# Reordering the attention blocks and the last product of a retention + mixture-of-experts kernel

## The chip, the cores and the metric

One core of one Trainium2 chip. The time is the device time of one execution in microseconds (us), median of several runs; lower is better. Distances inside an execution are taken from the start times in its trace.

## The reference

```python
def _attn_ref(q, k, v):                        # (8, 8, 576, 64) each
    scores = scale * np.matmul(q, k.transpose(0, 1, 3, 2))
    # Dmat[h, i, j] = gamma_h ** (i - j) for i >= j, else 0
    return np.matmul(scores * Dmat[None], v)

def _moe_ref(x, domain_probs, w1, w2):         # x: (4608, 512), 4 experts, F = 1024
    p = domain_probs / (domain_probs.sum(-1, keepdims=True) + 1e-09)
    out = 0
    for e in range(E):
        out += p[:, e:e + 1] * (np.maximum(x @ w1[e], 0.0) @ w2[e])
    return out
```

The result of attention, with its heads side by side, is the x of the experts.

## The kernel before

Attention is computed in chunks of 128 tokens with carried states: for a "duo" of two head pairs, `kv` builds the states of chunks from k^T v, `scores` the products inside a chunk, and `values` the output o, from the duo's own scores and from the states. A block takes the new duo's `kv` and `scores` and the old duo's `values`, so that VectorE and ScalarE have time between them. Blocks are set between the matmuls of the experts; ph is the result tile of their first layer, pd that of their second. The last 64 of the 576 tokens, the remainder, have products of their own (sr is the tile of their scores). A tile shape such as 128*64 is the rows and columns of TensorE's array that a matmul uses. Every result tile comes from one ring of four PSUM slots, two banks each.

```python
ring = ctx.enter_context(tc.tile_pool(name="ring", bufs=4, space=PSUM))
# ... class Duo:
def kv(self):
    kvp = ring_tile("kvp", [128, 2, NC, D])
    # ... 16 matmuls, tiles of 128*64: kvp += k^T v
    for j in range(2):
        r = slice(64 * j, 64 * j + 64)
        nc.scalar.activation(sbd[r, self.ps, :, r], kvp[r], Copy)     # the states
def scores(self):
    for i, p in self.pairs():
        s = ring_tile("s", [128, 2, NC, C])
        # ... 8 matmuls, tiles of 64*128; then one multiplication on VectorE: s -> sT
def values(self):
    o = ring_tile("o", [128, 2, SM])
    for i, p in self.pairs():                                         # own values, 128*64
        for c in range(NC):
            for j in range(2):
                nc.tensor.matmul(o[64*j:64*j+64, i, c*C:(c+1)*C], lhsT=bv[p][:, c, j, :],
                                 rhs=self.sT[p][:, j, c, :], start=(c == 0), stop=False, ...)
    for i, p in self.pairs():                                         # carried states, 128*128
        for c in range(1, NC):
            nc.tensor.matmul(o[:, i, c*C:(c+1)*C], lhsT=sbd[:, p, c-1, :],
                             rhs=self.qT[p][:, c, :], start=False, stop=(c == NC - 1), ...)
    # ... ScalarE copies o into xt, in two pieces
def block(new, old):
    if new is not None: new.kv()
    if old is not None: old.values()
    if new is not None: new.scores()
```

There are twelve duos: ten blocks with an old and a new duo, two with a new one only, two with an old one only.

The experts' second product goes by seven products and some sums for each group of 256 tokens. Its four result parts X, Y, W, Z lie in one ring tile `pd`: X and Y in one bank, W and Z in the other. The output rows of the group's second half are W + Y + p1 (left) and Y + p1 + p5 (right), with p1 and p5 copies of partial results.

```python
for m in (1, 4, 2, 5, 6, 3, 7):                # order of the products, every group
    d[s].product(m)
# ... in product(n), for the very last group:
elif n == 3:
    # ...
    if self.last:
        nc.gpsimd.tensor_tensor(self.p5, self.p5, self.p1, op=ADD)
        rd.append(nc.vector.tensor_tensor(self.ob[:, 0:HF], W, self.p1, op=ADD))
elif n == 7 and self.last:                     # both halves wait for Y, the last product
    nc.vector.tensor_tensor(self.ob[:, 0:HF], Y, self.ob[:, 0:HF], op=ADD)
    nc.sync.dma_start(out=out[n0 + 128:n0 + 256, 0:HF], in_=self.ob[:, 0:HF])
    nc.vector.tensor_tensor(self.ob[:, HF:Dm], Y, self.p5, op=ADD)
    nc.scalar.dma_start(out=out[n0 + 128:n0 + 256, HF:Dm], in_=self.ob[:, HF:Dm])
```

Of the kernel before, what the change touches and what calls it, by code (L numbers as in the profile page):

```python
# [9 lines left out]
FP32 = mybir.dt.float32  # L10
# [5 lines left out]
ADD = mybir.AluOpType.add  # L16
# [7 lines left out]
def kernel(  # L24
# [10 lines left out]
    nc = tc.nc  # L35
    B, H, S, D = q.shape
    N, E = moe_domain_probs.shape
    _, Dm, F = moe_w1.shape
    assert (B, H, S, D) == (8, 8, 576, 64) and (N, E, Dm, F) == (4608, 4, 512, 1024)
    scale = 1.0 / math.sqrt(D)  # L40
    C = 128
    NC = 4
# [7 lines left out]
    HF = Dm // 2  # L50
# [10 lines left out]
    opool = ctx.enter_context(tc.tile_pool(name="opool", bufs=2))  # L61
    tpool = ctx.enter_context(tc.tile_pool(name="tpool", bufs=1))
# [3 lines left out]
    def ring_tile(name, shape, dt=FP32):  # L66
        return ring.tile(shape, dt, tag="ring", name=name)
# [23 lines left out]
    sbd = const.tile([128, NP, NC, 128], BF16, name="sbd")  # L91
# [133 lines left out]
    def xt_of(t):  # L225
        if t not in xt:
            xt[t] = xpool.tile([128, NDC, NT], BF16, tag="xt", name="xt")
        return xt[t]


    class Duo:
        def __init__(self, b, d):
            self.b, self.d = b, d
            self.ps = slice(2 * d, 2 * d + 2)
            self.qT, self.kT, self.sT = {}, {}, {}
# [39 lines left out]
        def values(self):  # L275
            o = ring_tile("o", [128, 2, SM])
            for i, p in self.pairs():
                for c in range(NC):
                    for j in range(2):
                        nc.tensor.matmul(o[64 * j:64 * j + 64, i, c * C:(c + 1) * C], lhsT=bv[p][:, c, j, :],  # L280
                                         rhs=self.sT[p][:, j, c, :], start=(c == 0), stop=False, skip_group_check=True)
            for i, p in self.pairs():
                for c in range(1, NC):
                    nc.tensor.matmul(o[:, i, c * C:(c + 1) * C], lhsT=sbd[:, p, c - 1, :], rhs=self.qT[p][:, c, :],  # L284
                                     start=False, stop=(c == NC - 1), skip_group_check=True)
            n0 = self.b * S
            a = 0
            while a < SM:
                t = (n0 + a) // NT
                z = min(SM, (t + 1) * NT - n0)  # L290
                nc.scalar.activation(xt_of(t)[:, self.ps, n0 + a - t * NT:n0 + z - t * NT], o[:, :, a:z], Copy)
                a = z

    def block(new, old):
        if new is not None:
            new.kv()
        if old is not None:
            old.values()
        if new is not None:
            new.scores()  # L300


# [120 lines left out]
    class Down:  # L423


        def __init__(self, h, t, s):
            self.h, self.t, self.s = h, t, s
            self.last = t == n_nt - 1 and s == 1
            self.reads = [[], []]
            self.a = slice(256 * s, 256 * s + 128)  # L430
            self.b = slice(256 * s + 128, 256 * s + 256)

# [17 lines left out]
        def product(self, n):  # L450
            h = self.h
            if n == 1:
                self.ps = ring_tile("pd", [128, 2, 2, HF])
            X, Y, W, Z = (self.ps[:, 0, 0], self.ps[:, 0, 1], self.ps[:, 1, 0], self.ps[:, 1, 1])
            lo = range(KH)
            hi = range(KH, 2 * KH)
            A = {1: (X, True, h, lo, self.a, lambda c: wx[0][:, c, 0]),
                 2: (X, False, h, hi, self.a, lambda c: wx[1][:, c, 0]),
                 3: (Z, False, getattr(self, "s4", None), lo, slice(0, 128), lambda c: wx[1][:, c, 1]),
                 4: (W, True, h, hi, self.b, lambda c: t4w[:, c]),  # L460
                 5: (Z, True, getattr(self, "s1", None), lo, slice(0, 128), lambda c: wx[0][:, c, 1]),
                 6: (Y, True, getattr(self, "s2", None), lo, slice(0, 128), lambda c: t2w[:, c]),
                 7: (Y, False, h, lo, self.b, lambda c: t3w[:, c])}
            dst, start, src, ks, tok, rhs = A[n]
            bank = 0 if n in (1, 2, 6, 7) else 1
            for c, kk in enumerate(ks):
                mm = nc.tensor.matmul(dst, lhsT=src[:, kk, tok], rhs=rhs(c), start=(start and c == 0),  # L467
                                      stop=(c == KH - 1), skip_group_check=True)
                for r in self.reads[1 - bank]:
                    tc.declare_no_dep(mm.ins, r.ins, reason="another bank of the same tile")  # L470
            rd = self.reads[bank]
            n0 = self.t * NT + 256 * self.s
            if n == 1:
                self.p1 = tpool.tile([128, HF], FP32, tag="p1", name="p1")
                rd.append(nc.scalar.activation(self.p1, X, Copy))  # L475
            elif n == 2:
                self.oa = opool.tile([128, Dm], FP32, tag="o", name="oa")
                rd.append(nc.scalar.activation(self.oa[:, 0:HF], X, Copy))
            elif n == 5:
                self.p5 = tpool.tile([128, HF], FP32, tag="p5", name="p5")  # L480
                rd.append(nc.scalar.activation(self.p5, Z, Copy))
            elif n == 6:
                self.u = tpool.tile([128, HF], FP32, tag="uv", name="u")
                rd.append(nc.vector.tensor_tensor(self.u, Y, self.p1, op=ADD))  # L484
            elif n == 3:
                rd.append(nc.vector.tensor_tensor(self.oa[:, HF:Dm], Z, self.u, op=ADD))
                nc.sync.dma_start(out=out[n0:n0 + 128, :], in_=self.oa)
                if self.last:
                    self.ob = opool.tile([128, Dm], FP32, tag="o", name="ob")
                    nc.gpsimd.tensor_tensor(self.p5, self.p5, self.p1, op=ADD)  # L490
                    rd.append(nc.vector.tensor_tensor(self.ob[:, 0:HF], W, self.p1, op=ADD))
            elif n == 7 and self.last:
                nc.vector.tensor_tensor(self.ob[:, 0:HF], Y, self.ob[:, 0:HF], op=ADD)
                nc.sync.dma_start(out=out[n0 + 128:n0 + 256, 0:HF], in_=self.ob[:, 0:HF])
                nc.vector.tensor_tensor(self.ob[:, HF:Dm], Y, self.p5, op=ADD)
                nc.scalar.dma_start(out=out[n0 + 128:n0 + 256, HF:Dm], in_=self.ob[:, HF:Dm])
            elif n == 7:
                self.v = tpool.tile([128, HF], FP32, tag="uv", name="v")
                nc.vector.tensor_tensor(self.v, Y, self.p1, op=ADD)  # L499
                self.ob = opool.tile([128, Dm], FP32, tag="o", name="ob")  # L500
                nc.vector.tensor_tensor(self.ob[:, 0:HF], W, self.v, op=ADD)
                nc.gpsimd.tensor_tensor(self.ob[:, HF:Dm], self.v, self.p5, op=ADD)  # L502
                nc.sync.dma_start(out=out[n0 + 128:n0 + 256, :], in_=self.ob)
# [232 lines left out]
    def run(slots, i):  # L736
        for f in slots.get(i, []):
            f()

    slots = {}  # L740
    add = lambda i, f: slots.setdefault(i, []).append(f)
# [30 lines left out]
    n = 0  # L772
# [17 lines left out]
    NS = 30  # L790
# [5 lines left out]
    for b in range(2, B):  # L796
# [21 lines left out]
        for at, f in ((rem_at[1], rem.cast), (rem_at[1], rem.trans_dma), (rem_at[2], rem.scores), (rem_at[3], rem.values)):  # L818
            add(at, f)
    add(NS * 5 + 13, lambda old=old: block(None, old))  # L820

    for t in range(1, n_nt):
        d = [Down(h, t, s) for s in range(2)]
        for s in range(2):
            for i, which in enumerate((1, 2, 4, 3)):
                for lo in (0, KH // 2):
                    add(NS * (t - 1) + 16 + 7 * s + i,
                        lambda s=s, which=which, lo=lo, d=d: d[s].sums(which, lo, lo + KH // 2))
        n = NS * (t - 1)
        for e in range(E):  # L830
            for i in range(4):
                up_group(h, t, e, i)
                run(slots, n)
                n += 1
        for s in range(2):
            for m in (1, 4, 2, 5, 6, 3, 7):
                d[s].product(m)
                run(slots, n)
                n += 1
# [30 lines left out]
```

## Time and profile before

| kernel before | |
|---|---|
| time, median of 3 runs | 535.93 us (535.61 to 535.97) |
| profiled span | 533.7 us |
| a block: from the start of the expert matmul before it to the start of the one after it | 2.432 us (8 of the ten blocks) |
| the same where it stands between products of the second expert layer | 2.325 us (2 blocks) |
| first k^T v to last matmul | 421.67 us |
| tail: start of the last matmul to the end of the span | 3.96 us |

The two blocks between second-layer products are shorter because a matmul there is followed after 109 ns, not 216. The next lines are the chain of work that ended last, in order of time, around one block of before (start, length, engine, tile, line, count).

```profile
377.10 0.68 PE kvp L255 x16
377.78 0.45 PE o L280 x16
378.23 0.44 PE o L284 x6
378.67 0.55 PE s L269 x16
379.23 0.32 PE ph L359
```

### The profile page before, as it was taken

To read this page: it belongs to the slowest core of one execution; us is meant where nothing else is said; L and a number is where in the kernel's file an instruction comes from. 1 tells how busy PE (TensorE), PEld (TensorE's weight loads), DVE (VectorE), ACT (ScalarE), POOL (GpSimd) and SP (SyncE) were. 2 spreads that over 40 slices of the span, in tenths; PEclk is the share of its full clock that TensorE was granted. 3 is DMA by queue.
4 is the path that set the end of the run, shared out by engine and by line. 5 is a ranking of instruction groups with operands and counts; after the bars stand their busy time and mean duration, and the time that the engine had idled before them with its cause. 6 is when DMAs were issued, how large, how long until landed. Compare 5 with 4: busy or idle time off the path is not lost.

```text
span 533.7 us, 10188 instructions
## 1 busy us (share of the span) xinstructions
PE 525.1 (98%) x4221; PEld 340.4 (64%) x4260; DVE 362.1 (68%) x456; ACT 87.2 (16%) x175; POOL 147.1 (28%) x188
## 2 busy tenths in 40 slices
PE   8999999999999999999999999999999999999997
PEld 4644544478745885478646865587548844884586
DVE  5426668895577667697578767776765566556754
ACT  4723440012101111020101101100110000000010
POOL 5734104245235434336132514063000000000000
PEclk9999999999999999999999999999999999999999
DMA  9999947878769866937363655454011111110001
GB/s 238 208 212 251 238 116 190 166 164 168 155 146 170 169 139 146 165 73 164 106 136 93 142 140 115 104 120 124 20 41 31 50 39 41 41 46 14 1 32 49
DMA packets 145118, 63.55 MB, mean 119 GB/s; under 512 B 124240, under 2 KB 135888, under 8 KB 145072
## 3 DMA queue, kind: packets, MB, share of 16 engines
q1 hardware_dynamic: 134752, 43.50, 36.9%
q0 software_dynamic: 10176, 19.27, 16.5%
q8 instruction: 33, 0.54, 0.4%
q10 hardware_dynamic: 144, 0.13, 0.1%
q14 instruction: 13, 0.11, 0.1%
HBM read 53.56 MB, written 9.51 MB: 118 GB/s over the span
## 4 chain that ended last, share of the span: by engine, by line
PE 96%; DVE 1%; ACT 1%; DMA 1%; issue 1%; SPq 0%; DVEq 0%
PE ph L359 46%; PE pd L467 37%; PE po L394 5%; PE kvp L255 1%; PE o L280 1%; PE s L269 1%; PE o L284 1%; PE ph L380 1%; DMA raw_0q<-in_q_dram 1%; PE kvp L574 1%; PE w L138 1%; DVE h L365 0%; PE o L619 0%; ACT sbd L594 0%; PE pt L533 0%
## 5 line engine op out<-in xcount | busy, mean ns | idle before, releaser
L359 PE MATMUL ph<-xt,w 128*128 128x512 bf16 x1102 | 249.1, 379 | 2.0 <-DVE h L365 0.2
L365 DVE SCALAR_TENSOR_TENSOR h<-ph,pB 128x1024 bf16<-128x1024 f32 x128 | 156.5, 1224 | 56.9 <-PE ph L359 56.1
L359 PEld LDWEIGHTS <-w 128*128 128x128 bf16 x1136 | 109.3, 98 | 127.5
L467 PEld LDWEIGHTS <-h 128*128 128x128 bf16 x1024 | 99.8, 98 | 13.2
L467 PEld LDWEIGHTS <-s 128*128 128x128 bf16 x768 | 75.1, 98 | 8.6
L467 PE MATMUL pd<-wx,h 128*128 128x256 bf16 x512 | 61.1, 273 | 0.0
L467 PE MATMUL pd<-wx,s 128*128 128x256 bf16 x512 | 61.1, 273 | 0.0
L220 POOL DMA_DIRECT2D pB<-pd x28 | 15.8, 565 | 150.3 <-DVE h L365 134.7
L502 POOL TENSOR_TENSOR ob<-v,p 128x256 f32<-128x256 f32 x15 | 12.3, 822 | 114.2 <-DVE v L499 85.5
L239 POOL TENSOR_TENSOR bf_k<-raw_k,gk 128x512 bf16<-128x512 f32 x24 | 26.1, 1086 | 35.3 <-DMA raw_k<-in_k_dram 21.6
L260 ACT ACTIVATE sbd<-kvp 64x512 bf16<-64x512 f32 x24 | 14.2, 592 | 121.5 <-PE kvp L255 121.3
L271 DVE TENSOR_TENSOR sT<-s,tri 128x1024 bf16<-128x1024 f32 x24 | 28.3, 1219 | 7.5 <-PE s L269 7.5
L467 PE MATMUL pd<-t3w,h 128*128 128x256 bf16 x256 | 30.6, 273 | 0.0
L467 PE MATMUL pd<-t4w,h 128*128 128x256 bf16 x256 | 30.6, 273 | 0.0
L467 PE MATMUL pd<-t2w,s 128*128 128x256 bf16 x256 | 30.6, 273 | 0.0
L444 DVE TENSOR_TENSOR s<-s,h 128x1024 bf16<-128x1024 bf16 x32 | 29.6, 966 | 0.0
L394 PE MATMUL po<-wx,h 128*128 128x512 bf16 x124 | 28.6, 379 | 0.3 <-issue 0.2
L475 ACT ACTIVATE p<-pd 128x256 f32<-128x256 f32 x16 | 6.1, 384 | 138.9 <-PE pd L467 113.1
L239 POOL TENSOR_TENSOR bf_q<-raw_q,gq 128x512 bf16<-128x512 f32 x24 | 27.2, 1135 | 2.1 <-DMA raw_q<-in_q_dram 1.7
L448 DVE TENSOR_TENSOR s<-h,s 128x1024 bf16<-128x1024 bf16 x32 | 27.3, 891 | 0.0
L442 DVE TENSOR_TENSOR s<-h 128x1024 bf16<-128x1024 bf16 x32 | 23.5, 775 | 0.0
L484 DVE TENSOR_TENSOR u<-pd,p 128x256 f32<-128x256 f32 x16 | 6.8, 425 | 23.4 <-PE pd L467 23.3
(156 smaller groups left out, 370.2 us busy)
## 6 DMA issues: line engine op xcount, KB each, us to landing
pB<-pd POOLq DMA_DIRECT2D x28, 256.0 KB, 3.7
raw_k<-in_k_dram SPq DMA_DIRECT2D x48, 128.0 KB, 2.9
raw_q<-in_q_dram SPq DMA_DIRECT2D x48, 128.0 KB, 3.1
raw_v<-in_v_dram SPq DMA_DIRECT2D x48, 128.0 KB, 3.1
wx<-in_moe_w_dram POOLq DMA_DIRECT2D x4, 1024.0 KB, 15.4
out_dram<-oa SPq DMA_DIRECT2D x16, 256.0 KB, 2.2
out_dram<-ob SPq DMA_DIRECT2D x15, 256.0 KB, 2.2
w<-in_moe_w_dram POOLq DMA_DIRECT2D x3, 1024.0 KB, 15.1
```

What stands on the lines that cost most here:

```text
L220: eng.dma_start(out=pB[t, e], in_=pd[e:e + 1, t * NT:(t + 1) * NT].to_broadcast([128, NT]))
L239: eng.tensor_tensor(bfs[p % 2][n], raw1[n], g[:, :, 2 * p:2 * p + 2].unsqueeze(3).to_broadcast([128, NC, 2, D]), op=MULT)
L260: nc.scalar.activation(sbd[r, self.ps, :, r], kvp[r], Copy)
L271: nc.vector.tensor_tensor(sT[:, :, :, :].rearrange("p j c t -> p (j c) t"), s[:, :, :, :].rearrange("p j c t -> p (j c) t"), tri[:, :].uns ...
L359: nc.tensor.matmul(ph[:, f, :], lhsT=w1_sb[e][:, dc, fc * 128:(fc + 1) * 128], rhs=x[:, dc, :], start=(dc == 0), stop=(dc == NDC - 1))
L365: nc.vector.scalar_tensor_tensor(h[:, fk:fk + 2, :], ph, 0.0, pB[t, e][:, :].unsqueeze(1).to_broadcast([128, 2, NT]), op0=MAX, op1=MULT)
L394: nc.tensor.matmul(po[:, g, :], lhsT=h[:, e * NFC + fc, ns * 128:(ns + 1) * 128], rhs=wx[e // 2][:, (e % 2) * NFC + fc, :, :].rearrange("p ...
L442: nc.vector.tensor_tensor(self.alloc("s1")[:, l], h[:, l, self.b], h[:, r, self.b], op=ADD)
L444: nc.vector.tensor_tensor(self.alloc("s2")[:, l], self.s1[:, l], h[:, l, self.a], op=SUB)
L448: nc.vector.tensor_tensor(self.alloc("s4")[:, l], h[:, r, self.a], self.s2[:, l], op=SUB)
L467: mm = nc.tensor.matmul(dst, lhsT=src[:, kk, tok], rhs=rhs(c), start=(start and c == 0), stop=(c == KH - 1), skip_group_check=True)
L502: nc.gpsimd.tensor_tensor(self.ob[:, HF:Dm], self.v, self.p5, op=ADD)
```

## The change

The intent has two parts. In a block, let the states go first, since they have the tile shape of the expert matmuls before them: three changes of shape in place of four. At the very end, let the last product feed one half of one output only, so that one addition and one store follow it.

```diff
         def values(self):
             o = ring_tile("o", [128, 2, SM])
             for i, p in self.pairs():
+                for c in range(1, NC):
+                    nc.tensor.matmul(o[:, i, c * C:(c + 1) * C], lhsT=sbd[:, p, c - 1, :], rhs=self.qT[p][:, c, :],
+                                     start=(c == 1), stop=False, skip_group_check=True)
+            for i, p in self.pairs():
                 for c in range(NC):
                     for j in range(2):
                         nc.tensor.matmul(o[64 * j:64 * j + 64, i, c * C:(c + 1) * C], lhsT=bv[p][:, c, j, :],
-                                         rhs=self.sT[p][:, j, c, :], start=(c == 0), stop=False, skip_group_check=True)
-            for i, p in self.pairs():
-                for c in range(1, NC):
-                    ...
+                                         rhs=self.sT[p][:, j, c, :], start=False, stop=(c == NC - 1),
+                                         skip_group_check=True)
     def block(new, old):
-        if new is not None:
-            new.kv()
         if old is not None:
             old.values()
         if new is not None:
+            new.kv()
             new.scores()
# ... Down.product, last group only: Y in a ring tile of its own
+                if self.last:
+                    self.py = ring_tile("py", [128, HF])
+            if self.last:
+                Y = self.py
# ... the additions
-                if self.last:
-                    (GpSimd addition p5 + p1, VectorE addition W + p1)
             elif n == 7 and self.last:
-                (two additions of Y, each with a store)
+                self.v = tpool.tile([128, HF], FP32, tag="uv", name="v")
+                rd.append(nc.vector.tensor_tensor(self.v, Y, self.p1, op=ADD))
+                self.ob = opool.tile([128, Dm], FP32, tag="o", name="ob")
+                nc.vector.tensor_tensor(self.ob[:, HF:Dm], self.v, self.p5, op=ADD)
+                nc.scalar.dma_start(out=out[n0 + 128:n0 + 256, HF:Dm], in_=self.ob[:, HF:Dm])
+            elif n == 4 and self.last:
+                nc.vector.tensor_tensor(self.ob[:, 0:HF], W, self.v, op=ADD)
                 nc.sync.dma_start(out=out[n0 + 128:n0 + 256, 0:HF], in_=self.ob[:, 0:HF])
# ... the first sum of the last group three slots earlier, and the order of its products
-                    add(NS * (t - 1) + 16 + 7 * s + i,
+                    add(NS * (t - 1) + 16 + 7 * s + i - (3 if d[s].last and i == 0 else 0),
-            for m in (1, 4, 2, 5, 6, 3, 7):
+            for m in (1, 5, 2, 6, 3, 7, 4) if d[s].last else (1, 4, 2, 5, 6, 3, 7):
```

More of the change, by code (lines that the diff above doesn't have):

```diff
@@ L280, in values @@
                         nc.tensor.matmul(o[64 * j:64 * j + 64, i, c * C:(c + 1) * C], lhsT=bv[p][:, c, j, :],
-                                         rhs=self.sT[p][:, j, c, :], start=(c == 0), stop=False, skip_group_check=True)
-            for i, p in self.pairs():
-                for c in range(1, NC):
-                    nc.tensor.matmul(o[:, i, c * C:(c + 1) * C], lhsT=sbd[:, p, c - 1, :], rhs=self.qT[p][:, c, :],
-                                     start=False, stop=(c == NC - 1), skip_group_check=True)
+                                         rhs=self.sT[p][:, j, c, :], start=False, stop=(c == NC - 1),
+                                         skip_group_check=True)
             n0 = self.b * S
@@ L428, in __init__ @@
             self.last = t == n_nt - 1 and s == 1
-            self.reads = [[], []]
+            self.reads = [[], [], []]
             self.a = slice(256 * s, 256 * s + 128)
@@ L464, in product @@
             dst, start, src, ks, tok, rhs = A[n]
-            bank = 0 if n in (1, 2, 6, 7) else 1
+            bank = 2 if self.last and n in (6, 7) else 0 if n in (1, 2, 6, 7) else 1
             for c, kk in enumerate(ks):
@@ L468, in product @@
                                       stop=(c == KH - 1), skip_group_check=True)
-                for r in self.reads[1 - bank]:
+                for r in self.reads[1 - bank] if bank < 2 else ():
                     tc.declare_no_dep(mm.ins, r.ins, reason="another bank of the same tile")
@@ L487, in product @@
                 nc.sync.dma_start(out=out[n0:n0 + 128, :], in_=self.oa)
-                if self.last:
-                    self.ob = opool.tile([128, Dm], FP32, tag="o", name="ob")
-                    nc.gpsimd.tensor_tensor(self.p5, self.p5, self.p1, op=ADD)
-                    rd.append(nc.vector.tensor_tensor(self.ob[:, 0:HF], W, self.p1, op=ADD))
             elif n == 7 and self.last:
-                nc.vector.tensor_tensor(self.ob[:, 0:HF], Y, self.ob[:, 0:HF], op=ADD)
+                self.v = tpool.tile([128, HF], FP32, tag="uv", name="v")
[5 more added lines that the diff above has]
+                nc.vector.tensor_tensor(self.ob[:, 0:HF], W, self.v, op=ADD)
                 nc.sync.dma_start(out=out[n0 + 128:n0 + 256, 0:HF], in_=self.ob[:, 0:HF])
-                nc.vector.tensor_tensor(self.ob[:, HF:Dm], Y, self.p5, op=ADD)
-                nc.scalar.dma_start(out=out[n0 + 128:n0 + 256, HF:Dm], in_=self.ob[:, HF:Dm])
             elif n == 7:
```

## The prediction

> **What bounds the kernel now.** I read the page first (busy shares, then the chain that ended last), then the timeline of one block of attention products, then the last microseconds.
>
> ```profile
> PE 525.1 (98%) x4221; PEld 340.4 (64%) x4260; DVE 362.1 (68%) x456; ACT 87.2 (16%) x175; POOL 147.1 (28%) x188
> PE 96%; DVE 1%; ACT 1%; DMA 1%; issue 1%; SPq 0%; DVEq 0%
> ```
>
> TensorE (PE) is busy 98% and carries 96% of the chain. So only what shortens PE's stream, or the piece after its last matmul, can count. The number and shapes of the matmuls do not change; their order does. The next view is PE's timeline around one full block (columns: start, length, engine, line, operation, names, tile, shape, count).
>
> ```profile
> 376.29 0.81 PE L359 MATMUL ph<-xt,w 128*128 128x512 bf16 x3
> 377.03 0.75 PE L255 MATMUL kvp<-v,bf_k 128*64 128x256 bf16 x16
> 377.61 0.62 PE L280 MATMUL o<-sT,bf_v 128*64 128x128 bf16 x16
> 378.16 0.51 PE L284 MATMUL o<-qT,sbd 128*128 128x128 bf16 x6
> 378.60 0.62 PE L269 MATMUL s<-qT,kT 64*128 64x128 bf16 x16
> 379.16 0.39 PE L359 MATMUL ph<-xt,w 128*128 128x512 bf16 x1
> ```
>
> The reader is to see the tile column: 128*128, then 128*64 (k^T v and own values), then 128*128 (carried states), then 64*128 (scores), then 128*128: four changes of tile shape per block. In the trace's start times the matmul after each change comes late: k^T v 309 ns after a matmul that is otherwise followed after 216; states 151 after a pair usually 53 apart from the next; scores 152 after one usually 56; the next ph 148 after 53. Each change costs 93 to 98 ns, and the second step after it about 11 more. ScalarE (ACT) in the same block:
>
> ```profile
> 377.82 1.20 ACT L260 ACTIVATE sbd<-kvp 64x512 bf16<-64x512 f32 x2 [12.38 <-PE kvp L255]
> 379.04 1.08 ACT L291 ACTIVATE xt<-o 128x128 bf16<-128x128 f32 x2
> ```
>
> It first copies kvp into the state (done 379.02), then o into xt (done 380.13). PE's next ph at 379.16 is not held by either; note how narrow that is. How soon PE restarts on a released buffer is in two views, VectorE (DVE), then PE:
>
> ```profile
> 108.26 1.22 DVE L365 SCALAR_TENSOR_TENSOR h<-ph,pB 128x1024 bf16<-128x1024 f32 x1 [0.27 <-PE ph L359]
> ```
>
> ```profile
> 109.53 1.24 PE L359 MATMUL ph<-xt,w 128*128 128x512 bf16 x5 [0.15 <-DVE h L365]
> ```
>
> DVE ends at 109.483, PE starts at 109.535: 52 ns (other such places: 52 to 57). The end of the run, DVE, SyncE queue, ACT queue and DMA issues:
>
> ```profile
> 530.06 0.42 DVE L493 TENSOR_TENSOR ob<-pd,ob 128x256 f32<-128x256 f32 x1 [0.99 <-PE pd L467]
> 530.40 0.41 DVE L495 TENSOR_TENSOR ob<-pd,p 128x256 f32<-128x256 f32 x1
> ```
>
> ```profile
> 530.51 0.33 SPq L494 DMA_DIRECT2D out_dram<-ob  x1
> ```
>
> ```profile
> 530.85 0.37 ACTq L496 DMA_DIRECT2D out_dram<-ob  x1
> ```
>
> ```profile
> out_dram<-ob SPq DMA_DIRECT2D x1, 128.0 KB, 1.7
> out_dram<-ob ACTq DMA_DIRECT2D x1, 128.0 KB, 1.8
> ```
>
> Two half-row additions follow the last matmul, one after the other, each with its own 128 KB store. The second, issued at 530.85, lands near 532.6; about 1.1 us of closing work takes the span to 533.7.
>
> **What the Trainium skill says.** "TensorEngine Tiling (Array Packing)", Key Properties: changing the tiling mode (not just the tile) drains TensorE. The trace agrees and gives the price: 93 to 98 ns at each change, next to nothing between two products of one shape. "PSUM — Partial Sum Buffer", The four PSUM rules: the first matmul of a group clears the written-bits of a whole bank over the quadrants it writes, and later ones without that flag overwrite where the bit is clear. That makes the new start flags right: the states go first with start on chunk 1, and own values of chunk 0 then overwrite. No time is in it. "Perfetto Trace Analysis", Identifying the Most-Contended Engine: busy share says little about a pipelined TensorE; so I count start-to-start gaps, which the uneven gaps above support. Same page, DMA Instruction — HWDGE: a transfer's movement is not in the issuing instruction, and the final descriptor's wait for the write can be long; here 1.7 to 1.8 us from issue to landing.
>
> **The change, part by part.**
>
> 1. Order inside a block. New order: states (128*128), own values (128*64), k^T v (128*64), scores (64*128). The first shape is that of the product before the block, so three changes stay of four. Ten blocks have both an old and a new duo (twelve duos; two blocks have only a new one, two only an old one). From the old ph: states first at 0.216, last 5 x 56 ns later, 0.496; own values first at +0.149, 0.645, last 0.419 later, as in the old-only block at 396.9, 1.064; k^T v first 1.117, last 0.533 later, 1.650; scores first at +0.125, 1.775, last at +0.405, 2.180; next ph possible at +0.148, 2.328. Before it was 2.432 (376.725 to 379.157). Saved if nothing waits: 0.104 us, ten times 1.04 us.
>
> 2. But the blocks also allocate o before kvp now. The ring of result tiles has four slots and a block takes four (o, kvp, s, s), so the first product after it needs the slot that was kvp's and is now o's. The list of waits in the two built programs confirms it: the first ph after a block waited for the state copy and now waits for the second xt copy. o's last matmul starts at 1.064; in old-only blocks xt's copy starts 0.256 later (1.320); the two copies take 1.085 in every split (2.405); PE restarts 0.054 later: 2.459. That is 131 ns after the 2.328 where it could go, and 27 after the old 2.432. The slow second step (about 10 ns) is hidden by the wait. So a full block costs about +0.017 us instead of saving 0.104; ten give +0.17 us. Where a block sits between products of the down stage the next product also takes a ring slot: same sum. The state copies now end near 3.6, but the second ph after the block needs that slot only at about 2.46 + 8 x 0.216 = 4.19: no wait.
>
> 3. Old-only blocks (two): changes stay at two; about 0.015 us less each: -0.03.
>
> 4. Tail. The last product now feeds only W, so one addition of 0.42 us follows it and one store; Y's half is finished during the last product. The last store is issued where the first one was (530.51), not at 530.85. In the trace the first store is seen landed at 532.25, the second at 532.62: 0.37 us earlier. Y's own bank and the moved sums cost PE nothing, if the sums come in time: product 5 starts at 519.38 and its sum, moved up three slots, is done near 516.5; product 7 starts at 526.37 and its difference, queued behind an addition ending near 525.3, takes two halves of 0.64: first half 525.95, needed 526.37; second half 526.6, needed 527.24. The GpSimd addition that goes (0.73 us) was off the path.
>
> Sum: +0.17 - 0.03 - 0.37 = -0.23, so 535.93 becomes 535.70 us.
>
> **The rivals.** (a) The wait does not bind: 1.04 us from blocks, 0.37 from the tail, 0.03: 534.5. For it: ACT is only 16% busy. Against: the program's waits name the xt copy, and from o's last start to a free slot and a restarted PE it is 0.256 + 1.085 + 0.054 = 1.395 us, while PE has only 0.053 + 0.533 + 0.125 + 0.405 + 0.148 = 1.264 us of other work to do. (b) Something else stalls more: the scores now come 0.1 us sooner and need a slot that a DVE group frees. At 376.7 that group ends at 378.37, the second scores would start near 378.70; margin 0.3. If it bound, or the copies of ACT ran late, each block would lose 0.1 more: 536.7. (c) The tail's difference comes late and product 7 waits: up to 0.4 us, eating the tail's gain: 536.1. Against it the margins 0.4 and 0.6 above. (d) The first store was hidden by the closing work anyway: no gain in the tail, 536.1; against: the last SyncE waits follow the second landing directly.
>
> **Range and chances.** Between my sum and rival (a) lie 1.2 us, 0.2%; the three runs of before spread by 0.36. I take 535.7, with 534.9 to 536.1 eight times in ten; the lower side is longer for a part of (a). 2% would be 10.7 us, far beyond every rival: within 2% 0.98, faster 0.012, slower 0.008.
>
> **What would show it.** In PE's timeline a full block reads states, own values, k^T v, scores, with three late starts instead of four, about 0.10 us shorter from the old ph to the last score. The list of waits names ph (or pd) waiting for ACT's xt ten times, some 0.06 to 0.08 us idle each as PE's modelled ends count it. From the ph before a block to the ph after: about 2.46, not 2.33. The chain gains ACT xt. At the end one DVE addition follows the last matmul and its store is the last. I am wrong if that distance is 2.33 (rival a), if scores or product 7 start late (b, c), or if the last landing is not earlier (d).

## The result, and the profile after

| | before | after |
|---|---|---|
| median of 4 runs, same chip | 535.77 us (535.52 to 535.97) | 535.23 us (535.06 to 536.46) |
| ratio, 95% interval | | 0.9995 (0.9978 to 1.0012) |
| profiled span | 533.7 us | 533.7 us |
| first k^T v starts at | 108.08 us | 108.19 us |
| first k^T v to last matmul | 421.67 us | 421.95 us |
| tail | 3.96 us | 3.54 us |
| a block between ph matmuls (8) | 2.432 us | 2.459 us |

A ratio is the mean time of one kernel's runs over the mean time of the other's of the same rounds, so it is not quite the ratio of the medians. Executions over 1.5% slower than the fastest of the same kernel are left out of the means. The predicted 535.7 lies 0.5 us above the median. The run times alone do not say more: the interval of 0.34% is 1.8 us wide. In all the traces the first k^T v starts somewhere between 107.8 and 109.9 us, in a part of the program that the change does not touch. The rows under "first k^T v" leave that out, and they balance: 0.11 later, 0.28 longer in the middle, 0.42 shorter in the tail, which is -0.03 in the profiled span.

The page of after, busy shares and chain:

```profile
PE 526.5 (99%) x4260; PEld 342.4 (64%) x4260; DVE 361.7 (68%) x456; ACT 86.0 (16%) x175; POOL 144.5 (27%) x187
PE 73%; ACT 2%; DVE 0%; issue 0%
```

The 39 matmuls more than in before's page are records that before's trace lacks, not work. The chain is followed back only to 127.6 us, so its shares add up to 75%. ScalarE (ACT) has 2% of it: nine or ten pairs of copies of 1.09 us would be 1.8 to 2.0% of 533.7. The timeline of PE over the same block as in the prediction (start, length, engine, line, operation, names, tile, shape, count), then that of ACT:

```profile
377.31 0.50 PE L279 MATMUL o<-qT,sbd 128*128 128x128 bf16 x6
377.74 0.64 PE L284 MATMUL o<-sT,bf_v 128*64 128x128 bf16 x16
378.21 0.72 PE L255 MATMUL kvp<-v,bf_k 128*64 128x256 bf16 x16
378.87 0.62 PE L269 MATMUL s<-qT,kT 64*128 64x128 bf16 x16
379.56 0.81 PE L359 MATMUL ph<-xt,w 128*128 128x512 bf16 x3
```

```profile
378.42 1.08 ACT L292 ACTIVATE xt<-o 128x128 bf16<-128x128 f32 x2 [12.61 <-PE o L284]
379.39 1.19 ACT L260 ACTIVATE sbd<-kvp 64x512 bf16<-64x512 f32 x2
```

The shapes are now 128*128, 128*64, 128*64, 64*128, 128*128: one change less. By start times the states come 216 ns after the ph before them, the usual distance, and k^T v 53 ns after own values, the usual distance too. But the ph after the block comes 285 ns after the last score; a change of shape alone took 148 there before. ACT ends the copy of o at 379.51 and ph starts 0.05 later. The chain of after around this block says it outright:

```profile
377.81 0.59 PE o L284 x16
378.40 0.02 issue
378.42 1.09 ACT xt L292 x2
379.51 0.04 issue
379.56 5.34 PE ph L359 x24
```

Where before's chain ran on through kvp and s on PE, this one leaves PE after own values, goes through ACT's copy and returns at ph: k^T v and the scores are no longer on it. At the end of the run (timeline of all engines, then the last store's DMA issue with KB and us to landing):

```profile
528.50 1.91 PE L471 MATMUL pd<-t4w,h 128*128 128x256 bf16 x16
528.70 0.42 DVE L494 TENSOR_TENSOR v<-py,p 128x256 f32<-128x256 f32 x1 [0.91 <-PE py L471]
529.16 0.43 DVE L496 TENSOR_TENSOR ob<-v,p 128x256 f32<-128x256 f32 x1
529.62 0.37 ACTq L497 DMA_DIRECT2D out_dram<-ob  x1
530.45 0.42 DVE L499 TENSOR_TENSOR ob<-pd,v 128x256 f32<-128x256 f32 x1 [0.86 <-PE pd L471]
530.90 0.33 SPq L500 DMA_DIRECT2D out_dram<-ob  x1
```

```profile
out_dram<-ob SPq DMA_DIRECT2D x1, 128.0 KB, 1.7
```

Both additions for Y and the first store now lie beside the last product. One addition of 0.42 us and one store are left after it. Against before, whose two additions started at 530.06 and 530.40, the last matmul here starts 0.39 later, and the last store is seen landed at the same time (532.59 against 532.60).

### The profile page after: what moved, and what is told of

Read it like the earlier page. It is cut to its first block, busy times and chain, and to the rows that moved or that the text cites. A ratio compares the mean times of both kernels' runs of the same rounds, so it can differ in the third digit from the quotient of the medians.

```text
span 533.7 us, 10229 instructions
## 1 busy us (share of the span) xinstructions
PE 526.5 (99%) x4260; PEld 342.4 (64%) x4260; DVE 361.7 (68%) x456; ACT 86.0 (16%) x175; POOL 144.5 (27%) x187
## 4 chain that ended last, share of the span: by engine, by line
PE 73%; ACT 2%; DVE 0%; issue 0%
PE ph L359 37%; PE pd L471 34%; ACT xt L292 2%; PE o L284 1%; PE o L279 1%; PE py L471 1%; DVE h L365 0%; PE sr L338 0%; PE or L344 0%; PE or L346 0%; DVE ob L499 0%
## 5 line engine op out<-in xcount | busy, mean ns | idle before, releaser
L359 PEld LDWEIGHTS <-w 128*128 128x128 bf16 x1136 | 109.9, 98 | 127.9
L292 ACT ACTIVATE xt<-o 128x768 bf16<-128x768 f32 (+6 forms) x24 | 13.0, 594 | 116.8 <-PE o L284 116.8
L444 DVE TENSOR_TENSOR s<-s,h 128x1024 bf16<-128x1024 bf16 x32 | 31.2, 1013 | 0.0
L471 PE MATMUL pd<-t3w,h 128*128 128x256 bf16 x240 | 28.7, 273 | 0.0
L471 PE MATMUL pd<-t2w,s 128*128 128x256 bf16 x240 | 28.6, 273 | 0.0
L442 DVE TENSOR_TENSOR s<-h 128x1024 bf16<-128x1024 bf16 x32 | 24.8, 816 | 0.0
L448 DVE TENSOR_TENSOR s<-h,s 128x1024 bf16<-128x1024 bf16 x32 | 24.7, 811 | 0.0
```

The lines of the kernel that those rows point to most:

```text
L292: nc.scalar.activation(xt_of(t)[:, self.ps, n0 + a - t * NT:n0 + z - t * NT], o[:, :, a:z], Copy)
L359: nc.tensor.matmul(ph[:, f, :], lhsT=w1_sb[e][:, dc, fc * 128:(fc + 1) * 128], rhs=x[:, dc, :], start=(dc == 0), stop=(dc == NDC - 1))
L442: nc.vector.tensor_tensor(self.alloc("s1")[:, l], h[:, l, self.b], h[:, r, self.b], op=ADD)
L444: nc.vector.tensor_tensor(self.alloc("s2")[:, l], self.s1[:, l], h[:, l, self.a], op=SUB)
L448: nc.vector.tensor_tensor(self.alloc("s4")[:, l], h[:, r, self.a], self.s2[:, l], op=SUB)
L471: mm = nc.tensor.matmul(dst, lhsT=src[:, kk, tok], rhs=rhs(c), start=(start and c == 0), stop=(c == KH - 1), skip_group_check=True)
```

## The experiments

My theory: PE really saves about 0.10 us per block, but the product after the block takes the slot that ACT's copy of o frees, and this wait eats the saving and 0.027 us more; the tail gains about 0.4 us. The rivals: the change of shape saves less than I read; another wait (the scores' slots) holds the block; or the tail's gain is lost in a late sum or hidden by the closing work.

All outputs are right. Ratios are against before on the same chip in the same rounds. "Middle" is the distance from the first k^T v to the last matmul. Tail alone, blocks alone, states last, copies swapped stood beside a before of 535.51 us (median of 11 runs, one of them, of 1943.85, slow and left out of the ratio).

### 1. The tail alone

```diff
 # after, with values() and block() as in before
-        order in a block: states, own values, k^T v, scores
+        order in a block: k^T v, own values, states, scores
```

> The tail of the change alone, blocks as before. My theory: the full blocks stay at 2.43 us from the ph before to the ph after, and from the start of the last matmul to the end of the span it is about 3.5 us, against 3.96 us in the kernel before; so 0.35 to 0.45 us less, about 535.4 against 535.8. Rival (the first store was hidden, the tail gives nothing; the 0.5 us between the medians came from the blocks): 3.96 us again and no gain.

Measured: 535.13 us, ratio 1.0006 (0.9976 to 1.0037). A block takes 2.432 us and the middle 421.668, both as in before to the nanosecond that the trace gives; the tail is 3.551 in place of 3.960. So the tail's gain of 0.41 us is there without the blocks, and costs the middle nothing. The run times, 534.66 to 539.58, scatter too much to show it.

### 2. The blocks alone

```diff
 # after, with the last group as in before
-            for m in (1, 5, 2, 6, 3, 7, 4) if d[s].last else (1, 4, 2, 5, 6, 3, 7):
+            for m in (1, 4, 2, 5, 6, 3, 7):
 # ... and its additions, bank and sums as in before
```

> The block order alone, tail as before. My theory: three late starts instead of four, but the first product after the block waits for the copies of o, so 2.46 us per full block against 2.43: 0.2 to 0.3 us more in all, about 536.0. Rival (fewer changes of tile shape pay off): 2.33 us per block, 1.0 us less, 534.8.

Measured: 536.23 us, ratio 1.0009 (0.9990 to 1.0029). A block takes 2.460 us, as in after; the tail is 3.966, as in before. The middle is 422.137, 0.47 longer than before. Only about 0.2 of that is the blocks: one matmul of the remainder's scores (tile sr, near 172 us) started 478 ns after the matmul before it, where before has 216. That is a second wait, which experiment 7 returns to. The two parts of the change thus act apart, the tail -0.41 and the blocks +0.2.

### 3. The states last

If the theory holds, an order with three changes of shape that keeps kvp as the tile allocated and copied first collects the saving: k^T v, own values, scores, states. The states have the shape of the ph after them.

```diff
     def block(new, old):
-        if old is not None:
-            old.values()
         if new is not None:
             new.kv()
+        if old is not None:
+            old.own()
+        if new is not None:
             new.scores()
+        if old is not None:
+            old.carried()
```

`own` and `carried` are the two loops of `values`, with o allocated in the first and the copies in the second; the tail is that of after.

> Tail as in the changed kernel; in the block k^T v, own values, scores, states: also three changes of shape, but k^T v is first again, so the product after the block waits for the state copies, which end about 2.29 us after the ph before the block. My theory: about 2.35 us per full block (0.11 less than in the changed kernel, 0.08 less than before), no or a very short wait; 0.8 us less than before from ten blocks and 0.4 from the tail, near 534.6. Rival (changing the order gives nothing because something other than the copies holds the product after the block): 2.43 to 2.46 us per block, 535.3.

Measured: 534.43 us, ratio 0.9977 (0.9959 to 0.9994). Six of the eight blocks between ph matmuls take 2.370 to 2.373 us, two 2.415; the two others 2.249 and 2.310. That is 0.06 less than before for most, where 2.35 was expected. The start times tell where 22 ns stayed: the second scores start 73 to 77 ns after the first (52 usual), which is 53 ns after VectorE ends reading the tile that had their slot before. In the two blocks of 2.415 the ph after the states waits another 42 ns, about when ACT ends its state copies. So the change of shape is worth what I read, and with the copy of o off the path more than half of it is kept (0.06 of 0.104). Rival "another wait in the scores" exists here at 22 ns, but not in after, where the second scores follow at the usual distance.

### 4. The two copies swapped

The opposite test: after, with ACT doing the state copy before the copy of o. If ACT's first copy is what the next ph waits for, the wait must grow.

```diff
+        def copies(self):
+            o = self.o
             # ... the copies of o into xt
 # ... block:
         if new is not None:
             new.kv()
+        if old is not None:
+            old.copies()
+        if new is not None:
             new.scores()
```

> The changed kernel, its PE order untouched; only ScalarE's order in a block is turned round: state copies first, then the copies of o. The product after the block then waits for the state copies of a k^T v that ends later. My theory: k^T v's last matmul at 1.65, copies from 1.89 to 3.08, ph at 3.13 us: 0.67 us more per full block than the 2.46 of the changed kernel, ten times: 6.7 us, near 542. Rival (ScalarE does not hold PE): 2.46 us again and no difference.

Measured: 542.11 us, ratio 1.0120 (1.0098 to 1.0142): the interval does not touch 1. Six blocks take 3.125 us, two 3.198. PE, then ACT, in one of them:

```profile
386.06 1.24 PE L366 MATMUL ph<-xt,w 128*128 128x512 bf16 x5 [0.73 <-ACT sbd L260]
```

```profile
384.81 1.19 ACT L260 ACTIVATE sbd<-kvp 64x512 bf16<-64x512 f32 x2 [13.16 <-PE kvp L255]
386.03 1.09 ACT L296 ACTIVATE xt<-o 128x128 bf16<-128x128 f32 x2
```

The state copy ends at 386.00 and ph starts 0.06 later, so the wait for ACT's first copy sets the block's length; the rival, in which ScalarE does not hold PE, would have left 2.46. But the swap moved more than the time of a copy. The copies of o end only at 387.12, so this ph cannot be in o's slot, although o is still allocated first. The built programs agree: the first ph after a block gets o's slot in after, and kvp's here. So the next product gets the slot of the tile whose copy stands first in the program; the order of allocation does not decide it. Why two blocks take 3.198 was not looked into.

### 5. The copy of o in four pieces, in after and in before

A second test of the same wait: the copy alone is made longer. The second call stood beside a before of 536.52 us (535.34 to 540.92), a noisier chip.

```diff
-                nc.scalar.activation(xt_of(t)[:, self.ps, ...], o[:, :, a:z], Copy)
+                for i, p in self.pairs():
+                    nc.scalar.activation(xt_of(t)[:, p, ...], o[:, i, a:z], Copy)
```

After with it:

> The changed kernel with o copied in four pieces instead of two (one per pair and token piece), the same bytes. From pieces of the trace of before, a piece costs about 67 ns plus 0.83 ns per element, so the four take 0.13 us longer than the two. My theory: the product after a block waits for the last of them, so 2.59 us per full block instead of 2.46, 1.3 us more in all, near 536.6. Rival (the copies are not what PE waits for): 2.46 us.

Measured: 537.93 us, ratio 1.0010 (0.9952 to 1.0068), inconclusive. The profiled run was slow (783.09 us at a granted clock of 0.655), so its trace was not used. The same kernel once more, for its trace:

> The four pieces in the changed kernel once more, as the profile of its first submission fell into an execution at a granted clock of 0.655. Expected as before: 2.59 us per full block if the product after it waits for the copies, 2.46 if not.

Measured: one run, 536.97 us, state unknown, clock 1.000. A block takes 2.586 to 2.588 us. PE and ACT:

```profile
381.12 1.24 PE L360 MATMUL ph<-xt,w 128*128 128x512 bf16 x4 [0.20 <-ACT xt L293]
```

```profile
379.85 1.21 ACT L293 ACTIVATE xt<-o 128x64 bf16<-128x64 f32 x4 [12.61 <-PE o L284]
```

The copies take 1.21 in place of 1.08 us, 0.13 more, and the block takes 0.127 more (2.586 - 2.459): what the copy of o takes longer, the block takes longer. The control, before with the same four pieces:

> The control: the same four pieces in the kernel before, where the product after a block needs the slot of the state copies, which ScalarE does first. My theory: 2.43 us per full block as before, no change of time. Rival (more instructions of ScalarE cost PE time wherever they stand): some 0.13 us more per block here too.

Measured: 536.39 us, ratio 0.9989 (0.9932 to 1.0046). A block takes 2.432 us and the middle 421.672: no change. ACT is as slow here as in the other, and PE does not care. So it is the change that put ACT's copy on the path.

### 6. The tail taken apart: Y's bank, and the moved sum

After with Y left in X's bank:

```diff
-                if self.last:
-                    self.py = ring_tile("py", [128, HF])
-            if self.last:
-                Y = self.py
-            bank = 2 if self.last and n in (6, 7) else 0 if n in (1, 2, 6, 7) else 1
+            bank = 0 if n in (1, 2, 6, 7) else 1
```

> The changed kernel with Y left in X's bank, the product order of the tail kept. Product 6 then writes the bank that ScalarE still reads for oa, right after product 2: it should start about 0.6 us late (0.20 to the copy's start, 0.38 of copy, 0.05 to restart PE), so 0.6 us more, near 535.9. Rival (the bank of its own is not needed): no late start, no difference.

Measured: 535.71 us, ratio 0.9984 (0.9936 to 1.0032). In the timeline, ACT's copy of X and product 6:

```profile
523.24 0.38 ACT L478 ACTIVATE oa<-pd 128x256 f32<-128x256 f32 x1 [1.30 <-PE pd L467]
523.68 1.91 PE L467 MATMUL pd<-t2w,s 128*128 128x256 bf16 x16 [0.47 <-ACT oa L478]
```

Product 6 starts 744 ns after the last matmul of product 2, not 109: 0.635 us lost, as expected, while X is copied out of the bank. Without Y's own bank the new order of products would have cost more than the tail gains.

After with the first sum where it was:

```diff
-                    add(NS * (t - 1) + 16 + 7 * s + i - (3 if d[s].last and i == 0 else 0),
+                    add(NS * (t - 1) + 16 + 7 * s + i,
```

> The changed kernel with the first sum of the last token group left at its old place. It would end its first half near 519.8 and its second near 520.4, where product 5 starts at 519.8 and needs the second half 0.9 later: a late start of product 5 by at most 0.1 us, all else equal; within 0.1 us of the changed kernel. Rival (the sum holds product 5 for its whole length): 0.7 us or more.

Measured: 536.32 us, ratio 0.9992 (0.9944 to 1.0039). Sum and product 5 in the timeline:

```profile
520.34 1.64 DVE L442 TENSOR_TENSOR s<-h 128x1024 bf16<-128x1024 bf16 x2
```

```profile
521.44 1.81 PE L471 MATMUL pd<-wx,s 128*128 128x256 bf16 x15 [0.18 <-DVE s L442]
```

Product 5 starts 458 ns after the matmul before it, 0.35 us late; I had expected at most 0.1. My mistake was the length of the sum: I had used 0.64 us for a half, and here the two halves take 1.64, the first 1.04 and the second 0.68. The first half runs beside an addition that GpSimd (POOL) makes for the group before:

```profile
520.10 0.73 POOL L506 TENSOR_TENSOR ob<-v,p 128x256 f32<-128x256 f32 x1 [39.13 <-DVE v L503]
```

The Trainium skill, "SBUF — State Buffer", SBUF: two separate sides, says that a VectorE operation with two SBUF inputs and a GpSimd operation that reads SBUF exclude each other, the later one waiting. The trace of after agrees: of these sums and differences, the 78 halves (of 128) with no GpSimd work beside them take 676 to 686 ns; of the 50 with such work, 31 take 861 to 1580. So the move of the sum is needed. In after it is moved out of that neighbourhood, ends near 516.4 and is needed at 519.76.

### 7. After again, and the states last again

Beside a before of 535.60 us (535.28 to 537.62, 11 runs): the two kernels of interest in five rounds.

> The changed kernel once more, beside the next one on the same chip, because its first runs scattered by more than its gain. My theory: 0.2 to 0.4 us less than before; from the first k^T v to the last matmul 421.9 us against 421.7, from there to the end 3.54 against 3.96.

Measured: 536.28 us, ratio 0.9998 (0.9978 to 1.0018). The expected gain of 0.2 to 0.4 does not show. The trace says why the times cannot show it: the first k^T v starts at 109.87 us here, 1.7 us later than in the first trace of the same kernel, before anything that was changed. Tail (3.567) and blocks repeat. The middle is 422.31, 0.36 longer than in the other trace of after, and 0.356 of it is one place, the remainder's scores again:

```profile
174.67 0.28 PE L338 MATMUL sr<-qTr,kTr 128*128 128x64 bf16 x4 [0.28 <-DMA qTr<-bfr_q]
```

They wait for a DMA that transposes q and k. The wait of this tile over its usual 216 ns is 0 in before and in the tail alone, 82 ns in after, some 262 in the blocks alone, 433 in the states last, 438 here and 53 in the next run. In the five other traces that are read it is 0, and four of these have the block order of after, so that order alone does not set it. It also does not hide the blocks' cost: less this wait, and less the delays shown in experiment 6, the middle is 421.86 to 421.89 in after, the blocks alone, this run and both runs of experiment 6, against 421.67 in before. Why the transposes come late in some runs is open.

> The order k^T v, own values, scores, states once more on the same chip. My theory: 2.37 us per full block, 0.7 to 1.1 us less than before and 0.4 to 0.8 less than the changed kernel. Rival (its first result was the chip's mood): no difference from the changed kernel.

Measured: 534.57 us (534.16 to 534.82), ratio 0.9969 (0.9954 to 0.9985). The chain around the block:

```profile
376.33 0.68 PE kvp L255 x16
377.01 0.45 PE o L280 x16
377.46 0.59 PE s L269 x16
378.05 0.44 PE o L287 x6
378.49 0.22 PE ph L364
```

It stays on PE through all four products, as in before, with one change of shape less. The middle is 421.109; less its wait at sr of 0.053, 421.056, against 421.668 in before: 0.61 us. With 0.41 of the tail (3.547) that makes 1.02, and the medians differ by 1.03. Against after there is only this: the slowest of its six runs (534.82) is below the fastest of after (534.95).

## Why the prediction was right

The time and the class were right; so was the mechanism, but for the reason why the wait falls on o (step 2). That the time lies in the range says little by itself: rivals (c) and (d), at 536.1, lie within the scatter of the runs of after too (535.06 to 536.46). Step by step:

1. **Three shape changes in place of four.** Confirmed in the start distances (149, 53 and 125 ns inside the block, exactly those used) and in part collected where nothing waits for o (experiments 3 and 7).
2. **The wait for o's copy.** The predicted 2.459 us came out as 2.459 or 2.460 in all eight blocks between ph matmuls, and experiments 4 and 5 move it by moving or stretching the copy. Also as predicted, the slow second step after the block is gone (before's is 10 to 11 ns over the usual, after's is 215). Of the two blocks between second-layer products one took 2.352 (0.027 more than before, as predicted), the other, at 125 us, 2.412: ACT started its copy 0.32 us after o's last matmul in place of 0.26, behind a separate semaphore instruction of its own. That 0.06 was not foreseen. One reason was wrong, too: the prediction has the wait fall on o because o is now allocated before kvp. Experiment 4 leaves that order and lets ACT copy kvp first, and ph waits for kvp's copy. In the change both orders turn round together, so the wrong reason named the right slot; that was luck.
3. **Old-only blocks.** Predicted -0.03; they became shorter by 10 and 11 ns, but the second step after them is now 10 to 11 ns slow, since they end on 128*64. So zero.
4. **The tail.** Predicted -0.37, measured -0.42 (3.960 to 3.540); the tail alone -0.41. The estimate took the distance between two landings (0.37 in before's trace, from 532.23 to 532.60); what shrank is the whole distance from the last matmul to the end.
5. **The sum.** Predicted +0.14 from the blocks; the middle became 0.28 longer, of which 0.08 is the wait at sr that I had not seen, which leaves 0.20. With the tail that is -0.22 where I had -0.23. Two terms were off by 0.05 and 0.06 in opposite directions, so the sum is closer than its parts.

Of the rivals, (a) falls: 2.459, not 2.33. (b) falls in after, where the scores start at their usual distance. (c) falls: no late product in the tail of after, though experiment 6 shows what each part of the change prevents. (d) falls, though not by the sign that the prediction named: the last landing is not earlier (532.59 against 532.60), because the last matmul is later. Counted from the last matmul it is 0.40 us earlier, and the end of the span 0.42.

One of my tests was wrong. I wrote that the list of waits would name ph waiting for xt, 0.06 to 0.08 us each. It names none: counted from the modelled end of the scores (379.49), ph's idle time is 0.07 us, and no view of after marks it (they mark none under 0.15). A wait of 0.20 us (experiment 5) is marked. The chain and the start distances are what show the small one.

## What to carry to other kernels

When matmuls are reordered to save something on TensorE, look at which result tile is now the first that the next product needs back (here the one whose copy stands first in the program), and add up its path: last matmul, copy, restart; if that is longer than the work left for TensorE, the saving goes into a wait. Put the products whose result is copied by a slow engine so that this copy is not the one the next product waits for. And where run times scatter by more than the effect, read distances between start times inside the trace, from a point after which nothing else differs.

## What the Trainium skill lacked or had wrong

- "TensorEngine Tiling (Array Packing)", Key Properties, says that a change of mode drains TensorE but gives no price. Here each change between 128*128, 128*64 and 64*128 tiles cost 93 to 100 ns (the most from k^T v to the scores, 125 against 25), and the second step after it 10 to 11 more (226 against 216, 120 against 109).
- "ScalarE: Activation LUTs", What ACT_TABLE_LOAD costs, gives 186 ns fixed for an activation with immediates and an overlap of 93 back to back, so by an estimate from that page each further piece of a copy adds 93 ns. Here two further pieces of the copy of o added 0.13 us (1.21 against 1.08), some 63 ns each. The page does not say in which memory its tile lay; this copy reads PSUM.
- No page that I read has the time from the release of a result buffer to TensorE's next start on it: 50 to 57 ns in the traces of before and after.
- "Perfetto Trace Analysis", Identifying the Most-Contended Engine, warns that the busy share of TensorE is a bad measure of how near a kernel is to its limit, as matmuls are pipelined. It does not say that the idle time before a matmul is as bad a measure of waits: with a wait of about 137 ns per block (285 less 148), the idle time by modelled ends is 0.07 us and no wait was listed.
